# First weight loads on a second queue, scales of three weight chunks from Gram products, and one feed-forward piece in two groups

## The chip, the cores and the metric

The kernel runs on one core of a Trainium2 chip. Its time is device time in microseconds (us): the median of several executions, and before the change three of them gave 1026.77 to 1027.06. A core has five engines that work through their own instruction streams in order: TensorE (PE in the profile; PEld is its weight load), VectorE (DVE), ScalarE (ACT), GpSimd (POOL) and SyncE (SP), which issues most of the DMA transfers. Engines wait for one another by semaphores.

## What is computed

Block-causal attention over 8 batches, 8 heads and 576 positions with heads of 64 (a block of 64 rows sees itself and all blocks before it), and then a feed-forward layer over its output, 4608 tokens of 512.

```python
scores = scale * np.matmul(q, k.transpose(0, 1, 3, 2))
mask = block_i >= block_j                      # blocks of 64
attn = softmax(np.where(mask, scores, -1e9))
x = (attn @ v).transpose(0, 2, 1, 3).reshape(4608, 512)
h = x @ w_in                                   # 512 x 2048
g = h * np.clip(h + 3.0, 0.0, 6.0) / 6.0
out = (g @ w_out).astype(np.float32)           # 2048 x 512
```

q, k and v are float32; the two weight matrices are float64.

## The kernel before

**Precision.** TensorE multiplies fp16 numbers. Nearly every operand is scaled by a power of two, so that its largest element fits, and split into a high and a low fp16 half; a product is three matmuls (high by high, high by low, low by high). The first part of the work is done in plain float32 instead: the attention of batch 0's first 192 rows and the feed-forward of those 192 tokens, since the scales are not known yet.

**Weights.** They come in eight chunks, four loads each (two of `w_in`, two of `w_out`, 512 KB each). A load brings float64 as pairs of 32-bit words into a raw buffer; ScalarE makes `ex` out of the high word, VectorE shifts the low word into `sg` and joins both into float32 in `win` or `wout` (`w_load`, line 605). `w_max` (646) takes the largest magnitude of each chunk: four ScalarE passes with Abs and a running maximum, a transposition on TensorE that brings the 128 partial maxima into a row, a reduction, and a matmul that spreads the result (`pow2_scale`, 529). Its exponent gives the chunk's scale, `pwio`, and the reciprocal, `rsio`. `w_split` (659) writes the two fp16 halves over the float32 of the chunk before. The raw buffers rotate among three places; the constants WX and WY say when the third changes.

**Attention.** A slot is a pair of heads of one batch, 32 in all. Slots 0 to 3 (batch 0) begin in float32 (`qk_prep32`, `s_block32`, `t_block32`, `pv_group32`; tiles `qf`, `qkf`, `sf`, `pf`); the others go through `qk_prep` (767), which takes the absolute maximum of q and k on VectorE (`qkmx`), `s_group` (scores `s`, maxima `st`, exponentials `p`, halves `phl`, transposed by DMA into `pT`) and `pv_group` (1111), which writes the feed-forward's input `x`, one of four buffers `xb`.

**Feed-forward.** 13 pieces: 192 tokens (piece 0), 384, 384, 192, and then nine of 384. A piece has 16 blocks of 128 hidden units. `ffn1_` (1193) makes `h` in one of two PSUM banks, ScalarE's relu gives `r`, VectorE and ScalarE make the two halves of `g`; `ffn2_` (1249) adds g @ w_out to three accumulators `o`, three blocks (LAG) later, and evicts them as `osb` after the sixteenth. The relu needs the scales `eg` (`g_scales`, 674) and `sh` (`h_scale`, 741): they are normed by the largest product of scales over **all eight** chunks. So the relu of piece 1's first block, the first one in fp16, needs the maximum of the last chunk (`need`, 1351, calls `maxes(NCH)`).

**Order.** Nothing above runs in the order of the code. A recorder collects every operation with the tiles it touches (`Recorder.touch`, 195) and a key, a due time out of a table of constants: AS and RT for the float32 slots, AT for the others, FT for the feed-forward, W0 and WD for the weight loads, M0 and MD for the chunk maxima, S0 and SD for the splits. A list scheduler with a cost model (`cost`, 216, `schedule`, 271) then gives each engine its order, and chooses the engine where an operation has several (`scaled` with "AVP"). `emit` (459) issues the instructions, so nearly all carry that line in the trace, and groups are told apart by their tiles.

Of the kernel before, what the change touches and what calls it, by code (L numbers as in the profile page):

```python
# [22 lines left out]
WX = 10  # L23
WY = 27

U = 2.788
AS = (7.494, 11.408, 15.3, 22.633)
AL = 14.807
PV0 = 2.519
TA, TR, PR = 2.197, 5.661, 0.677  # L30
QR = 3.417
PVA, PVB = 0.93, 1.25
# [8 lines left out]
MEM = 0  # L41

NMIN = 64
QL = 0.849
VL = 0.2
W0, WD = 4.938, 2.891
S0, SD = 57.576, 4.59
M0, MD = 34.073, 5
RT = (25.619, 42.369, 59.881, 71.242)
RS, RL, VL1 = 2.796, 15.216, 24.0  # L50
VM0, VMX = 10.452, 0.3
AT = ((4, 86.25), (6, 128.63), (8, 159.32), (10, 199.92), (12, 240.31), (14, 287.79), (16, 335.13), (24, 565.96), (32, 826.62))
# [31 lines left out]
class Recorder:  # L84
# [75 lines left out]

    def load(self, out, in_):

        self.add([(e, "dma_start", (out, in_), {}) for e in self.queues])

    def add(self, ways):
# [8 lines left out]
        else:  # L174
# [15 lines left out]
            self.ops.append(op)  # L190
        for a, w in [(a, False) for a in ins] + [(a, True) for a in outs]:
            if self.on_chip(a):
                self.touch(op, a, w)

    def touch(self, op, a, w):
# [9 lines left out]
        keep = []  # L205
        for e in self.hist.get(t.name, ()):
            o, ow, q0, q1, c0, c1 = e
            inside = p0 <= q0 and q1 <= p1 and b0 <= c0 and c1 <= b1
            if o is not op and (w or ow) and q0 < p1 and p0 < q1 and c0 < b1 and b0 < c1:
                op.preds[o.n] = op.preds.get(o.n, False) or ow and not w  # L210
            if not (w and inside):
                keep.append(e)
        keep.append((op, w, p0, p1, b0, b1))
        self.hist[t.name] = keep

    def cost(self, eng, method, args, kw, outs, ins):
# [3 lines left out]
        if method == "dma_start":  # L220
# [8 lines left out]
            return 600, 2000 + nb / 170, False  # L229
# [41 lines left out]
    def schedule(self):  # L271
# [63 lines left out]
        while done < N:  # L335
# [131 lines left out]
def kernel(  # L467
# [61 lines left out]
    def pow2_scale(mx, n, nm, to=None, exact=False):  # L529
# [26 lines left out]
        nc.vector.tensor_scalar_mul(rs, pw, 1.0 / E_IN)  # L556
        nc.vector.reciprocal(rs, rs)
# [46 lines left out]

    def w_load(w, c, half):
# [52 lines left out]

    def w_split(c):

        rs = rsio[:, c]
        for wi, w in enumerate("io"):
            for half in range(2):
                c32 = w_f32(w, c, half)
                part = w_part(w, c, half)
                hi, lo = (part[:, :, i].rearrange("p r (l n) -> p r l n", l=2) for i in range(2))
                nc.scaled(hi, c32, rs[:, wi:wi + 1], "AVP")
                nc.vector.scalar_tensor_tensor(
                    lo, c32, rs[:, wi:wi + 1], hi, op0=ALU.mult, op1=ALU.subtract
                )  # L670

    gs = []

    def g_scales():

        if not gs:
            pp = sm.tile([P, NCH], F32, tag="pp", name="pp")
            nc.vector.tensor_mul(pp, pwi, pwo)
            m = wpool.tile([P, 1], F32, tag="egm", name="egm")
# [802 lines left out]
```

## Time and profile before

| | |
|---|---|
| median of 3 runs | 1026.9 us (1026.77 to 1027.06) |
| profiled execution, its own time | 1024.76 us |
| span of its profile | 1023.0 us |
| mean granted clock of TensorE | 0.992 |

| engine | busy us | share of the span |
|---|---|---|
| TensorE | 988.8 | 97% |
| VectorE | 821.9 | 80% |
| ScalarE | 624.8 | 61% |
| GpSimd | 61.5 | 6% |

The span runs from the first instruction to the last of the profiled execution. The busy time by stage is cut at the places where TensorE stops being full: the start until 42 us, a gap at 72 to 81, a gap at 128 to 158; behind that TensorE stays busy to the end. Each such row has the stage, its length, then for PE, PEld, DVE, ACT and POOL the busy time and (x) the number of instructions, and at the end the granted clock, the DMA share and GB/s. A row of an engine's timeline has start and length in us, the operation, out<-in, the shapes, and in brackets the idle time ahead of it and what ended that.

### The profile page before, as it was taken

What the parts mean: (1) busy time and instruction counts of PE and PEld (TensorE: products, weight loads), DVE (VectorE), ACT (ScalarE), POOL (GpSimd) and SP (SyncE); (2) the same over time, 40 slices, a digit from 0 to 9 for tenths busy, and PEclk for the clock granted to TensorE, in tenths of its full rate; (3) what the DMA queues carried; (4) which work ended last, traced back from release to release, by engine and by line L of the source; (5) the groups of instructions that cost most, each with busy time, mean ns of one, the idle gap of its engine ahead of it and who ended that gap; (6) DMA issues with size and microseconds to landing.
All of it is one profiled execution on the core that took longest, in us unless ns stands there. A gap on an engine that the chain in (4) does not pass through costs nothing. (4 is left out here: it accounts for less than half of the span.)

```text
span 1023.0 us, 28975 instructions
## 1 busy us (share of the span) xinstructions
PE 988.8 (97%) x11588; PEld 727.2 (71%) x11588; DVE 821.9 (80%) x2311; ACT 624.8 (61%) x1525; POOL 61.5 (6%) x247
## 2 busy tenths in 40 slices
PE   7889989999999999999999999999999999999998
PEld 4656647677777877677767677677777777777776
DVE  4898999999999999998999999887988774232322
ACT  4688766567667766677776675665665653343332
POOL 3211110000000000000000000000000000000000
PEclk9998998999999999999999999999999999999999
DMA  6767755989989998798779788775566352000000
GB/s 157 206 184 210 173 130 97 169 167 182 160 149 180 155 170 162 131 189 145 141 159 159 137 158 155 132 139 90 103 143 103 70 100 35 1 33 2 32 2 32
DMA packets 414200, 128.91 MB, mean 126 GB/s; under 512 B 403184, under 2 KB 403440, under 8 KB 414064
## 3 DMA queue, kind: packets, MB, share of 16 engines
q1 hardware_dynamic: 414064, 127.05, 64.3%
q8 instruction: 91, 1.49, 0.6%
q14 instruction: 45, 0.37, 0.1%
HBM read 45.09 MB, written 9.44 MB: 53 GB/s over the span
## 5 line engine op out<-in xcount | busy, mean ns | idle before, releaser
L463 PE MATMUL h<-x,win 128*64 128x384 f16 (+2 forms) x4720 | 435.9, 321 | 6.2 <-DVE win L463 3.6
L463 PE MATMUL o<-wout,g 128*64 128x512 f16 (+2 forms) x3444 | 428.7, 378 | 0.0
L463 PEld LDWEIGHTS <-win 128*64 128x64 f16 x4608 | 297.6, 110 | 68.6 <-issue 1.7
L463 PEld LDWEIGHTS <-g 128*64 128x64 f16 x3360 | 222.6, 110 | 101.9
L463 ACT ACTIVATE p<-s,st,esc 128x64 f32<-128x64 f32 (+1 forms) x280 | 163.1, 586 | 71.7 <-DVE st L463 56.4
L463 ACT ACTIVATE r<-h,eg,sh 128x384 f32<-128x384 f32 (+1 forms) x240 | 137.2, 592 | 105.7 <-PE h L463 102.9
L463 DVE SCALAR_TENSOR_TENSOR r<-r,eg,h 128x384 f32<-128x384 f32 (+1 forms) x192 | 113.4, 591 | 107.7 <-ACT r L463 107.5
L463 ACT ACTIVATE g<-r 128x384 f16<-128x384 f32 (+1 forms) x163 | 83.2, 511 | 91.2 <-DVE r L463 90.2
L463 DVE SCALAR_TENSOR_TENSOR phl<-p,st,phl 128x128 f16<-128x128 f32 (+4 forms) x252 | 134.9, 582 | 0.2
L463 DVE SCALAR_TENSOR_TENSOR g<-r,g 128x384 f16<-128x384 f32 (+1 forms) x192 | 102.9, 536 | 30.4 <-ACT g L463 29.6
L463 DVE TENSOR_REDUCE st<-s 128x1 f32<-128x64 f32 (+1 forms) x280 | 119.8, 447 | 4.7 <-PE s L463 4.7
L463 PE MATMUL s<-qkT 128*64 128x64 f16 (+7 forms) x1120 | 98.7, 289 | 3.9 <-ACT p L463 2.9
L463 ACT ACTIVATE phl<-p,st 128x256 f16<-128x256 f32 (+4 forms) x122 | 64.2, 556 | 39.6 <-DVE st L463 15.2
L463 PEld LDWEIGHTS <-vhl 128*64 128x64 f16 x1680 | 72.8, 111 | 21.3 <-issue 13.0
L463 PEld LDWEIGHTS <-qkT 128*64 128x64 f16 x1120 | 60.2, 111 | 32.3 <-issue 10.4
L463 PE MATMUL pv<-pT,vhl 128*64 128x192 f16 (+2 forms) x1680 | 74.6, 235 | 8.3 <-DMA pT<-phl 3.2
L463 ACT ACTIVATION_READ_ACCUMULATOR p<-s,st,esc 128x1 f32 x280 | 54.9, 196 | 0.0
L463 POOL MEMSET p<- 128x64 f32 x140 | 21.3, 152 | 518.0 <-DVE phl L463 474.3
L463 DVE TENSOR_SCALAR phl<-p,st 128x512 f16<-128x512 f32 (+4 forms) x130 | 50.0, 418 | 1.7 <-issue 0.3
L463 DVE SCALAR_TENSOR_TENSOR qks<-qk,rs_q,qks 128x576 f16<-128x576 f32 x56 | 44.0, 810 | 0.1
L463 ACT ACTIVATE x<-pv 128x192 f16<-128x192 f32 (+1 forms) x66 | 24.0, 364 | 30.8 <-PE pv L463 27.5
L463 DVE TENSOR_REDUCE qkmx<-qk 128x2 f32<-128x1152 f32 x28 | 37.6, 1344 | 0.8 <-DMA qk<-in_k_dram 0.8
(147 smaller groups left out, 785.5 us busy)
## 6 DMA issues: line engine op xcount, KB each, us to landing
out_dram<-osb SPq DMA_DIRECT2D x35, 256.0 KB, 2.5
vnat<-in_v_dram SPq DMA_DIRECT2D x64, 128.0 KB, 2.8
qk<-in_q_dram SPq DMA_DIRECT2D x28, 288.0 KB, 3.5
qk<-in_k_dram SPq DMA_DIRECT2D x28, 288.0 KB, 4.4
rawo<-in_moe_w_out_dram SPq DMA_DIRECT2D x15, 512.0 KB, 4.0
rawi<-in_moe_w_in_dram SPq DMA_DIRECT2D x14, 512.0 KB, 3.7
pT<-phl SPq DMA_TRANSPOSE x140, 3.5
vnat<-in_v_dram SPq DMA_DIRECT2D x32, 32.0 KB, 2.6
```

The source lines that it names most:

```text
L463: getattr(eng, method)(*args, **kw)
```

## The change

- **Loads.** The first four loads (chunk 0) may go on SyncE's or ScalarE's queue (WQ); the scheduler puts all four on ScalarE's. The table RAWS names the raw buffer of each load, out of six places; the first ten turn through five of them, parts of `xb` among these.
- **Maxima.** For chunks 0 to 2 (GRM) `w_max` no longer uses ScalarE: TensorE multiplies the bf16 upper halves of the float32 weights with themselves (16 matmuls of 128x128 for a chunk, tile `gm`), VectorE takes the diagonal (sums of squares, `wm`), a matmul with ones adds these up (`gs`), and half of that sum's exponent bounds the largest element. Chunks 3 to 7 take two Abs passes of 1024 columns in place of four of 512.
- **Piece 1** is cut into two groups of blocks (GA = 5): the first ten blocks use scales made of chunks 0 to 4 alone; after the tenth the accumulators are evicted into `sofar`, and the last six blocks' result is added to it. `need` asks for five chunk maxima ahead of piece 1, and for all eight ahead of its eleventh block.
- **Shorter chains.** The factor 1/E_IN now comes from the matmul with `one`, so `pow2_scale` and `h_scale` have one VectorE operation less each.
- **Other engines.** The absolute maximum of q and k of slots below 8 (QKA) may go to ScalarE, and the scaled identity `rd` to ScalarE or GpSimd (RDW).
- **Scheduler.** `touch` keeps reads and writes apart; DMA costs are changed; nearly all keys have new values.

Order rows of both kernels follow, at two places. They have the line, the operation, out<-in and the shape; the number behind a tile's name is its allocation.

First place, the program's start, on TensorE. Before (`qt` are transpositions of q and k of the first slot, `sf` its scores):

```order
L463 MATMUL qt_0_110<-ident,qf_106 128x128
L463 MATMUL qt_0_110<-ident,qf_106 128x64
L463 MATMUL qt_1_109<-ident,qf_106 128x128
L463 MATMUL qt_1_109<-ident,qf_106 128x64
L463 MATMUL sf_0_0_116<-qkf_108 128x128
L463 MATMUL sf_1_0_127<-qkf_108 128x128
L463 MATMUL sf_2_0_142<-qkf_108 128x192
L463 MATMUL qt_0_123<-ident,qf_120 128x128
```

In the changed kernel the transpositions of slot 0 and chunk 0's Gram matmuls come first. The last three of these (each with a weight load) and what follows:

```order
L483 LDWEIGHTS wout
L483 MATMUL gm_236<-wout 128x128
L483 MATMUL sf_0_0_119<-qkf_112 128x128
L483 MATMUL qt_1_123<-ident,qf_121 128x128
L483 MATMUL qt_1_123<-ident,qf_121 128x64
L483 MATMUL qt_0_124<-ident,qf_121 128x128
L483 MATMUL qt_0_124<-ident,qf_121 128x64
L483 MATMUL sf_1_0_130<-qkf_112 128x128
```

The first scores (`sf_0_0`) have moved from the place behind four transpositions to that behind the sixteen Gram matmuls, which read the assembled `win` and `wout` of chunk 0.

ScalarE at the same place. Before (`qkf` are the evicted transpositions, `pf` the exponentials):

```order
L463 ACT_TABLE_LOAD
L463 ACTIVATE qkf_108<-qt_0_110 64x3x64
L463 ACTIVATE qkf_108<-qt_1_109 128x192
L463 ACTIVATE pf_0_117,sums_0_114<-sf_0_0_116,st_0_115 128x64
L463 ACTIVATE qkf_121<-qt_0_123 64x3x64
L463 ACTIVATE pT_0_124<-pt_0_0_125 128x128
```

And now:

```order
L483 DMA rawi_0_104<-in_moe_w_in_dram 128x2x512
L483 DMA rawi_1_107<-in_moe_w_in_dram 128x2x512
L483 DMA x_82<-in_moe_w_out_dram 128x1024
L483 DMA x_83<-in_moe_w_out_dram 128x1024
L483 ACT_TABLE_LOAD
L483 ACTIVATE exi_0_106<-rawi_0_104 128x512
L483 ACTIVATE exi_1_109<-rawi_1_107 128x512
L483 ACTIVATE qkf_112<-qt_0_114 64x3x64
L483 ACTIVATE exo_0_116<-x_82 128x512
L483 ACTIVATE exo_1_128<-x_83 128x512
L483 ACTIVATE qkf_112<-qt_1_113 128x192
L483 ACTIVATE qkf_122<-qt_1_123 128x192
```

Four DMA issues (`x_82` and `x_83` are raw buffers in `xb`) stand ahead of the table load, and four `ex` passes stand among the evictions `qkf`.

Second place, VectorE where the scales of piece 1 are made. Before, chunk 7's maximum ends in `am_w`, `pwio` and `rsio`, and `egm`, `rpp`, `eg` and `sh` follow it:

```order
L463 TENSOR_TENSOR pp<-pwio 128x8
L463 RECIPROCAL rsio<-rsio 128x2
L463 TENSOR_REDUCE egm<-pp 128x1
L463 TENSOR_SCALAR win<-x_83,rsio 128x2x256
L463 RECIPROCAL rpp<-egm 128x1
L463 TENSOR_SCALAR wout<-x_84,rsio 128x512
L463 TENSOR_SCALAR eg<-pp,rpp 128x8 x3
L463 SCALAR_TENSOR_TENSOR sh_636<-pwio,pw_v_186,eg 128x8
L463 SCALAR_TENSOR_TENSOR win<-x_83,rsio,win 128x2x256
L463 TENSOR_SCALAR sh_636<-sh_636 128x8
L463 SCALAR_TENSOR_TENSOR win<-x_83,rsio,win 128x2x256
L463 SCALAR_TENSOR_TENSOR wout<-x_84,rsio,wout 128x512
```

Now these operations have 5 columns and come once chunk 4 is done:

```order
L483 TENSOR_SCALAR eg_588<-pp_586,rpp_589 128x5
L483 TENSOR_SCALAR x_82<-rb_2_493,rs_v_188 128x192
L483 TENSOR_SCALAR eg_588<-pp_586,rpp_589 128x5
L483 SCALAR_TENSOR_TENSOR x_82<-rb_2_493,rs_v_188,x_82 128x192
L483 TENSOR_SCALAR am_w_474<-mb_w_477 128x2
L483 TENSOR_SCALAR eg_588<-pp_586,rpp_589 128x5
L483 TENSOR_SCALAR pwio<-am_w_474 128x2
L483 SCALAR_TENSOR_TENSOR sh_5_590<-pwio,pw_v_187,eg_588 128x5
L483 RECIPROCAL rsio<-pwio 128x2
L483 SCALAR_TENSOR_TENSOR so_5_760<-pw_v_187,egm_587 128x1
```

Eleven rows are left out; behind them the scores of slot 4 (`s_0_0_0`) begin:

```order
L483 TENSOR_SCALAR wout<-wout,rsio 128x512
L483 TENSOR_TENSOR sums_2_487<-sums_2_487,st_8_524 128x1
L483 SCALAR_TENSOR_TENSOR wout<-wout,rsio 128x512
L483 TENSOR_SCALAR sums_2_487<-sums_2_487 128x3
L483 TENSOR_REDUCE st_0_551<-s_0_0_0_552 128x1
L483 RECIPROCAL sums_2_487<-sums_2_487 128x3
L483 TENSOR_REDUCE st_0_551<-s_0_0_0_552 128x1 x2
```

Before, slot 4's first three score maxima stood some 80 rows ahead of `sh`; now they stand behind it.

The diff, cut to its core:

```diff
-WX = 10
-WY = 27
+RAWS = (0, 1, 3, 4, 5) * 2 + (0, 1, 4, 5) * 3 + (0, 1, 2) * 2 + (0, 1) * 2
...
+WSP = 2
+LOW = "V"
+WQ = 4
+GA = 5
+GRM = 3
+QKA = 8
+RDW = "PA"
...
-S0, SD = 57.576, 4.59
-M0, MD = 34.073, 5
+S0, SD = 66.989, 3.661
+M0, MD = 32.413, 7.476
...
-        nc.vector.tensor_scalar_mul(rs, pw, 1.0 / E_IN)
-        nc.vector.reciprocal(rs, rs)
+        nc.vector.reciprocal(rs, pw)
...
-        b = len(n_raw) % 3 if len(n_raw) < WY else len(n_raw) % 2
+        b = RAWS[len(n_raw)]
...
+            raw = flat(xb[b - 2], I32)[:, :2 * WC].rearrange("p (n w) -> p n w", w=2)
         n_raw.append(nm)
+        nc.queues = ("sync", "scalar") if len(n_raw) <= WQ else ("sync",)
...
     def w_max(c):
 
-        acc = sm.tile([P, 2, 2], F32, tag="wacc", bufs=2, name=f"wacc{c}")
+        if c >= GRM:
+            m = sm.tile([P, 2], F32, tag="wm", name=f"wm{c}")
+            for wi, w in enumerate("io"):
+                c32 = w_all32(w, c)
+                ab = ffp.tile([P, WC], F32, tag="stage", bufs=NST_B, name=f"ab{w}{c}").bitcast(BF16)
+                ab = ab.rearrange("p (r l n) -> p r l n", r=c32.shape[1], l=2)
+                nc.scalar.activation(ab, c32, AF.Abs, accum_out=m[:, wi:wi + 1])
+            pow2_scale(m, 2, f"w{c}", (pwio[:, c], rsio[:, c]), exact=True)
+            return
+        ps = ps_s.tile([P, 512], F32, tag="s", name=f"gm{c}")
+        nc.joint = "gm", c
         for wi, w in enumerate("io"):
-            for half in range(2):
-                c32 = w_f32(w, c, half)
-                ab = ffp.tile([P, WC], F32, tag="stage", bufs=NST_B, name=f"ab{w}{c}_{half}")
-                ab = ab.rearrange("p (r l n) -> p r l n", r=c32.shape[1], l=2)
-                nc.scalar.activation(ab, c32, AF.Abs, accum_out=acc[:, wi, half:half + 1])
+            t = w_all32(w, c).rearrange("p r l n -> p (r l n)").bitcast(BF16)
+            t = t.rearrange("p (n w) -> p n w", w=2)[:, :, 1]
+            nk = 2 * WC // P
+            for k_ in range(nk):
+                tk = t[:, k_ * P:(k_ + 1) * P]
+                nc.tensor.matmul(ps[:, wi * P:(wi + 1) * P], tk, tk, start=k_ == 0, stop=k_ == nk - 1)
+        nc.joint = None
         m = sm.tile([P, 2], F32, tag="wm", name=f"wm{c}")
-        nc.vector.tensor_reduce(m, acc, axis=AX.X, op=ALU.max)
-        pow2_scale(m, 2, f"w{c}", (pwio[:, c], rsio[:, c]), exact=True)
+        dg = sm.tile([P, P], F32, tag="wdg", bufs=1, name=f"wdg{c}")
+        for wi in range(2):
+            nc.vector.tensor_tensor_reduce(
+                dg, ps[:, wi * P:(wi + 1) * P], ident, 1.0, 0.0,
+                op0=ALU.mult, op1=ALU.add, accum_out=m[:, wi:wi + 1],
+            )
+        ps2 = ps_s.tile([P, 512], F32, tag="s", name=f"gs{c}")
+        nc.joint = "gs", c
+        for h in range(2):
+            nc.tensor.matmul(ps2[h * BLK:(h + 1) * BLK, :2], full1, m, start=True, stop=True)
+        nc.joint = None
+        u = sm.tile([P, 2], F32, tag="wu", name=f"wu{c}")
+        nc.vector.tensor_scalar(
+            u.bitcast(U32), ps2[:, :2].bitcast(U32), 1, EXPONENT_BITS,
+            op0=ALU.logical_shift_right, op1=ALU.bitwise_and,
+        )
+        nc.vector.tensor_scalar(pwio[:, c], u, 2.0 ** 64 / E_IN, TINY, op0=ALU.mult, op1=ALU.max)
+        nc.vector.reciprocal(rsio[:, c], pwio[:, c])
...
+            for r in range(0, R, R // WSP):
+                rr = slice(r, r + R // WSP)
+                nc.scaled(hi[:, rr], c32[:, rr], rs[:, wi:wi + 1], "AVP")
+                nc.resid(lo[:, rr], c32[:, rr], rs[:, wi:wi + 1], hi[:, rr], LOW)
...
+    def g_scales(n=NCH):
...
+            nc.vector.tensor_mul(pp, pwi[:, :n], pwo[:, :n])
...
+    def g_group(pc, f):
+
+        return GA if pc == 1 and f * NCH // NFT < GA else NCH
...
-        absmax(mx, t)
+        ways = [("vector", "tensor_reduce", (mx, t), dict(axis=AX.XY, op=ALU.max, apply_absolute_value=True))]
+        if n < QKA:
+            ways.append(("scalar", [
+                ("activation", (sp[:, 2].rearrange("p t l d -> p (t l d)")[:, :NST * D].rearrange("p (t d) -> p t d", d=D), t[:, s], AF.Abs), dict(accum_out=mx[:, s:s + 1]))
+                for s in range(2)
+            ]))
+        nc.add(ways)
...
-            nc.gpsimd.tensor_scalar(rd[:, i], ident2, r[:, i:i + 1], 1.0, op0=ALU.mult, op1=ALU.mult)
+            nc.scaled(rd[:, i], ident2, r[:, i:i + 1], RDW)
...
+        cut = not last and g_group(pc, f) != g_group(pc, f + 1)
+        first = first or g_group(pc, f) != g_group(pc, f - 1)
+        last = last or cut
...
+        if cut:
+            so = out_scales(pc, g_group(pc, f))
+            for t, a in enumerate(acc[pc]):
+                nc.scaled(sofar[:, t], a, so[:, t:t + 1], "AV")
+            acc[pc] = [ps_o.tile([P, DM], F32, tag=f"o{t}", name=f"o{pc}_{t}b") for t in range(nt)]
...
+            if pc == 1 and GA < NCH:
+                nc.vector.scalar_tensor_tensor(
+                    oc, ac, so[:, t:t + 1], sofar[:, t], op0=ALU.mult, op1=ALU.add
+                )
+            else:
+                nc.scaled(oc, ac, so[:, t:t + 1] if pc else 1.0 / 6.0, "AV")
...
-        maxes(NCH)
+        maxes(NCH if pc > 1 or c >= GA else GA)
```

More of the change, by code (lines that the diff above doesn't have):

```diff
@@ L159, in scaled, with resid @@
         self.add(ways)
+    def resid(self, out, in_, scale, hi, engines):
+        self.add([
+            ("vector" if e == "V" else "gpsimd", "scalar_tensor_tensor", (out, in_, scale, hi),
+             dict(op0=ALU.mult, op1=ALU.subtract))
+            for e in engines
+        ])
     def load(self, out, in_):
@@ L190, in add @@
             self.ops.append(op)
+        for _, *call in ways[1:]:
+            for _, a, k in call[0] if isinstance(call[0], list) else [call]:
+                more, _ = self.operands(a, k)
+                outs = outs + [x for x in more if all(x is not y for y in outs)]
         for a, w in [(a, False) for a in ins] + [(a, True) for a in outs]:
@@ L204, in touch @@
             op.tiles.append(t.name)
[L205 to L214, printed above, removed]
+        writes, reads = self.hist.setdefault(t.name, ([], []))
+        for kind in (writes, reads) if w else (writes,):
+            keep = []
+            for e in kind:
+                o, q0, q1, c0, c1 = e
+                if o is not op and q0 < p1 and p0 < q1 and c0 < b1 and b0 < c1:
+                    op.preds[o.n] = op.preds.get(o.n, False) or kind is writes and not w
+                if not (w and p0 <= q0 and q1 <= p1 and b0 <= c0 and c1 <= b1):
+                    keep.append(e)
+            if w:
+                kind[:] = keep
+        (writes if w else reads).append((op, p0, p1, b0, b1))
     def cost(self, eng, method, args, kw, outs, ins):
@@ L603, in w_f32, with w_all, w_all32 @@
         return t.rearrange("p (r l n) -> p r l n", r=NDT // 2 if w == "i" else 1, l=2)
+    def w_all(w, c):
+        if w == "i":
+            return win[:, c]
+        return wout[:, 2 * c:2 * c + 2]
+    def w_all32(w, c):
+        if c + 1 < NCH:
+            return w_all(w, c + 1).bitcast(F32)
+        t = flat(xb[2 if w == "i" else 3], F32)[:, :2 * WC]
+        return t.rearrange("p (r l n) -> p r l n", r=NDT if w == "i" else 2, l=2)
     def w_load(w, c, half):
@@ L662, in w_split @@
         for wi, w in enumerate("io"):
[L663 to L679, printed above, removed]
+            c32 = w_all32(w, c)
+            part = w_all(w, c)
+            hi, lo = (part[:, :, i].rearrange("p r (l n) -> p r l n", l=2) for i in range(2))
+            R = c32.shape[1]
+            for r in range(0, R, R // WSP):
+                rr = slice(r, r + R // WSP)
+                nc.scaled(hi[:, rr], c32[:, rr], rs[:, wi:wi + 1], "AVP")
+                nc.resid(lo[:, rr], c32[:, rr], rs[:, wi:wi + 1], hi[:, rr], LOW)
+    gs = {}
+    def g_scales(n=NCH):
+        if n not in gs:
+            pp = sm.tile([P, n], F32, tag=f"pp{n}", bufs=1, name=f"pp{n}")
+            nc.vector.tensor_mul(pp, pwi[:, :n], pwo[:, :n])
+            m = wpool.tile([P, 1], F32, tag=f"egm{n}", name=f"egm{n}")
             nc.vector.tensor_reduce(m, pp, axis=AX.X, op=ALU.max)
-            t = wpool.tile([P, 3, NCH], F32, tag="eg", name="eg")
-            r = sm.tile([P, 1], F32, tag="rpwi", name="rpp")
+            t = wpool.tile([P, 3, n], F32, tag=f"eg{n}", name=f"eg{n}")
+            r = wpool.tile([P, 1], F32, tag=f"rpp{n}", name=f"rpp{n}")
             nc.vector.reciprocal(r, m)
@@ L1128, in pv_group @@
             if pc in (2, 3):
[L1129 removed]
+                need(NPC, NCH - 1)
         t = pT.pop((n, g))
```

91 lines of the change are left out of this document (46 added, 45 removed).

## The prediction

> **What bounds the kernel now.** I read the page's first lines, then cut the span into stages by their busy times, then read each engine's timeline where a stage shows TensorE idle. The page's totals first.
>
> ```profile
> span 1023.0 us, 28975 instructions
> ...
> PE 988.8 (97%) x11588; PEld 727.2 (71%) x11588; DVE 821.9 (80%) x2311; ACT 624.8 (61%) x1525; POOL 61.5 (6%) x247
> ```
>
> TensorE (PE) is idle for 1023.0 - 988.8 = 34.2 us in all, so a change that keeps its work cannot gain much more than that, plus what a throttled clock costs. The busy time by stage (length, then PE, PEld, DVE, ACT, POOL busy, then granted clock, DMA share, GB/s) says where those 34 us lie.
>
> ```profile
> 0.00:5.80 5.80, 1.65 (x4) 0.75 (x5) 1.31 (x7) 1.94 (x3) 4.77 (x19) 1.00 0.33 75
> 5.80:14.00 8.20, 7.40 (x24) 4.83 (x24) 3.69 (x12) 3.26 (x17) 2.67 (x12) 1.00 0.45 102
> 14.00:28.00 14.00, 11.96 (x48) 7.63 (x48) 6.91 (x21) 6.11 (x26) 2.67 (x7) 1.00 0.92 247
> 28.00:42.00 14.00, 11.26 (x69) 7.47 (x66) 11.41 (x36) 11.29 (x34) 3.12 (x8) 1.00 0.77 205
> 42.00:72.00 30.00, 29.74 (x178) 19.37 (x176) 28.20 (x75) 23.72 (x62) 5.74 (x11) 1.00 0.63 184
> 72.00:81.00 9.00, 4.08 (x16) 2.81 (x18) 8.08 (x19) 7.17 (x19) 0.72 (x1) 0.69 0.66 195
> 81.00:128.00 47.00, 46.95 (x303) 31.18 (x299) 43.45 (x119) 37.43 (x98) 8.85 (x21) 0.99 0.74 189
> 128.00:147.00 19.00, 16.77 (x121) 9.71 (x123) 18.92 (x66) 12.97 (x36) 2.43 (x7) 0.91 0.61 136
> 147.00:158.00 11.00, 6.35 (x71) 4.03 (x66) 11.00 (x36) 8.05 (x18) 1.72 (x4) 0.81 0.60 128
> 158.00:400.00 242.00, 239.44 (x3312) 183.69 (x3313) 239.79 (x718) 163.34 (x407) 11.22 (x62) 0.99 0.90 158
> ...
> 840.00:1010.00 170.00, 169.58 (x1868) 128.90 (x1864) 56.69 (x103) 61.64 (x117) 0.00 (x0) 1.00 0.08 18
> ```
>
> Three places hold most of it. The **start** (0 to 42) leaves PE idle for 4.15 + 0.80 + 2.04 + 2.74 = 9.7 us. **Hole B** (72 to 81) has 4.92 us idle and, at a clock of 0.69, loses another 9 x 0.31 = 2.8 us: 7.7 us. **Hole A** (128 to 158) has 2.23 + 4.65 us idle and 19 x 0.09 + 11 x 0.19 = 3.8 us of clock: 10.7 us. From 158 to 400 PE and VectorE (DVE) are both full, DVE for 239.79 of 242; from 840 on PE runs alone. So the end is PE's work plus these holes, and an earlier arrival at 158 is kept.
>
> **What the holes wait for.** TensorE's timeline (start, length; in brackets the idle time before it and what ended it), then VectorE's and ScalarE's (ACT):
>
> ```profile
> 75.38 1.65 PE L463 MATMUL h<-x,win 128*128 128x192 f32 x4 [3.56 <-DVE win L463]
> 78.57 1.01 PE L463 MATMUL h<-x,win 128*128 128x192 f32 x2 [1.54 <-DVE g L463]
> ...
> 155.12 1.40 PE L463 MATMUL s<-qkT 128*64 128x64 f16 x16 [1.65 <-ACT p L463]
> ```
>
> ```profile
> 74.65 0.67 DVE L463 SCALAR_TENSOR_TENSOR win<-exi,sgi 128x512 uint32<-128x512 uint32 x1
> ...
> 143.71 0.40 DVE L463 SCALAR_TENSOR_TENSOR x<-rb,rs_v,x 128x192 f16<-128x192 f32 x1
> ...
> 155.17 0.22 DVE L463 SCALAR_TENSOR_TENSOR sh<-pwio,pw_v,eg 128x8 f32<-128x8 f32 x1
> ```
>
> ```profile
> 140.14 0.62 ACT L463 ACTIVATE abo<-x 128x512 f32<-128x512 f32 x1
> ...
> 156.17 1.23 ACT L463 ACTIVATE r<-h,eg,sh 128x384 f32<-128x384 f32 x2 [0.34 <-DVE sh L463]
> ```
>
> Hole B: the f32 feed-forward of piece 0 waits for the assembly of chunk 3's weights (`win`), which DVE ends at 75.3. Hole A: the first relu of piece 1 waits for `sh`, the scales that need the maxima of all eight chunks; the last maximum starts on ScalarE at 140.14, and its chain through PE and DVE ends at 156.2. Piece 1's input x was complete at 143.71 + 0.40 = 144.1. Both `h` banks are held meanwhile, so PE has only scraps of attention to run.
>
> **The change part by part.** *Hole A.* The scales of piece 1's first ten blocks need chunks 0 to 4 alone, and they now stand in DVE's order ahead of slot 4's scores (the second place shown with the change). The 16 us chain leaves the path. Next late is x: the relu could start about 2 us after 144.1, 10 us earlier. The chain's own part is the stage from 147 to 158, 4.65 us of idle time and 2.1 us of clock; of the 3.9 us before it, waits for a loaded DVE, I take half. -8.7 us (bounds 0 and -10.7).
>
> *Hole B.* Chunk 3's assembly moves ahead in DVE's order: 35 us of DVE work stand before it where there were 50, summed from the start-to-start times of before. The wait of 3.56 us and the slow clock behind it go; next late is `g`, whose 1.54 us may stay in part. -7.0 us (bounds -3 and -7.7).
>
> *Start.* Four weight loads leave SyncE's queue and stand on ScalarE's, ahead of its table load, and chunk 0's 16 Gram matmuls stand in PE's order ahead of the first scores (the first place). Behind the waiting Gram matmuls are the scores, and so the exponentials; on ScalarE the q and k evictions queue behind `exo`, on DVE behind `win`.
>
> ```profile
> 5.81 1.83 PE L463 MATMUL sf<-qkf 128*128 128x128 f32 x6 [0.47 <-issue]
> ```
>
> ```profile
> rawi<-in_moe_w_in_dram SPq DMA_DIRECT2D x14, 512.0 KB, 3.7
> ```
>
> Four loads are 2.1 MB; the first 14 us of before moved 5.8 x 75 + 8.2 x 102 = 1.3 MB of q, k and v. At the 247 GB/s of 14 to 28 the weights alone take 8.5 us, all of it 13.8 us. With 0.7 us until the first issue and 3.2 us for prelu, assembly and Gram (an estimate: 0.7 + 0.7 + 1.8), the first scores come at 12.4 to 17.7, against 5.81. I take 14.4, 8.6 us late. Part is made up: between 14 and 42 PE had 4.8 us of idle time and DVE was busy for 18.3 of 28 us. +4.5 us (bounds -2, if earlier loads shorten that stretch as well, and +16, if nothing is made up and the rate is worse).
>
> The Trainium skill (Trainium Kernel Development and Optimization, Key Constraints) says that the queues of several engines share the same 16 DMA engines and save only issue time. By that rule, which speaks against this move, ScalarE's queue brings no bandwidth, and the q, k and v loads slow down beside it. No run here shows two queues yet.
>
> *Gram work.* 48 matmuls of 128x128 in bf16 have no row. Between these lies their price:
>
> ```profile
> 105.70 0.82 PE L463 MATMUL pt<-ident,pf 128*128 128x128 f32 x6
> 106.35 0.82 PE L463 MATMUL h<-x,win 128*128 128x192 f32 x4
> ...
> 857.46 2.15 PE L463 MATMUL h<-x,win 128*64 128x384 f16 x24
> 859.41 2.14 PE L463 MATMUL o<-wout,g 128*64 128x512 f16 x18
> ```
>
> An f32 pass of 128 columns takes 0.65 / 6 = 0.11 us. In f16, 24 halves of 384 columns take 1.95 us, 0.16 us for a full array, so 0.05 us for 128 columns. 2.6 to 5.2 us; being 16 bit, nearer to the low end: 3.0, less 0.7 us for three transposed maxima: +2.3 us (bounds 1.9 and 4.5).
>
> *The cut in piece 1, and the shorter chains.*
>
> ```profile
> L463 ACT ACTIVATE osb<-o,so 128x512 f32<-128x512 f32 x28 | 18.2, 687 | 5.9 <-PE o L463 5.7
> L463 DVE TENSOR_REDUCE qkmx<-qk 128x2 f32<-128x1152 f32 x28 | 37.6, 1344 | 0.8 <-DMA qk<-in_k_dram 0.8
> L463 DVE TENSOR_SCALAR rs_q<-pw_q 128x2 f32<-128x2 f32 x28 | 4.4, 156 | 0.1
> ```
>
> Three more evictions of 0.69 us stand between the tenth block's output and the next group's. In PE's order a whole `h` block of 1.95 us lies between and hides them: +0.5 us; without that cover 2 us. DVE loses 28 x 0.156 us of `rs_q`, four `qkmx` of 1.34 us and some 50 small ones, about 16 us, and gains about 5 us (Gram diagonals, a second set of scales, piece 1's sums). ScalarE takes some of it over and is at 61%. In the stage from 158 to 400, where DVE is full, PE idles for 2.56 us: -1.0 us (bounds -2.6 and +1).
>
> **The sum**: -8.7 - 7.0 + 4.5 + 2.3 + 0.5 - 1.0 = -9.4 us. The profiled execution took 1024.76 us (the span of 1023.0 and 1.8 around it), which gives 1015.4. The median of the runs lies 2.1 us above that execution: 1017.5.
>
> **Rivals.** *1, slower: the start comes too late.* If the five-buffer loads share badly and get two thirds of 247 GB/s, 3.4 MB take 20.6 us, the first scores come at 24.5, 18.7 us late, and none of it is made up, since the f32 slots 0 to 3 follow one another through the same tiles. 18.7 + 2.3 + 0.5 - 16.7 = +4.8: 1031.7. It decides from a first score near 20 on. For it: at 247 GB/s the DMA share is 0.92 already, and three engines queue behind these loads. Against it: one load alone lands 3.7 us after its issue.
>
> *2, no change: paid back.* The start loses its 8.6 us in full, Gram 4.5, the cut 2, while Hole A shrinks by 8 and Hole B by 7: about 0, 1027. For it: DVE was busy for 18.92 of 19 us ahead of 147, so PE may meet DVE where it met `sh`. Against it: DVE has less to do before that point.
>
> *3, a smaller gain: a cold PE.*
>
> ```profile
> 8.77 0.45 PE L463 MATMUL pt<-ident,pf 128*128 128x128 f32 x1 [0.32 <-ACT pf L463]
> ...
> 29.46 0.27 PE L463 MATMUL pt<-ident,pf 128*128 128x128 f32 x1
> ```
>
> One transposition takes 0.45 us early and 0.27 us later: PE starts slow, though the first stages' rows say 1.00. If the wait before the Gram matmuls keeps it slow for 10 us more, 5 us go: 1022.5. The Trainium skill (TensorE: Matmul & The Clock Gate, Part 1) states half rate after an idle window of about 3.4 us. The trace agrees in Hole B, 3.56 us of waiting and a clock of 0.69.
>
> **How the numbers follow.** Forecast 0.64, rival 1 0.12, rival 2 0.13, rival 3 0.11. A measurement of this kernel can tell about 0.2%, 2 us, from no change. Forecast and rival 3 are faster (0.75), rival 2 is the same (0.13), rival 1 slower (0.12). The forecast's own range is 1008 to 1023. The low end of mine, 1005, puts the better bounds of all terms together; the high end, 1028, takes in rivals 2 and 3 and leaves rival 1 out.
>
> **What would show it.** In the changed profile: first scores between 12 and 18; no wait of `h` for `win` above 1 us; a first relu of piece 1 before 150, not ended by `sh`; PE idle for about 28 us; from 840 on the same 1.95 us for a block. A first score past 20, a new PE wait of several us around piece 1's start or its cut, or DVE idle for more than 5 us between 160 and 400 would make me wrong.

## The result

| | median us | runs | lowest to highest us | ratio to before (95% interval) |
|---|---|---|---|---|
| before | 1026.98 | 4 | 1026.77 to 1027.61 | |
| changed | 1011.55 | 4 | 1009.56 to 1014.19 | 0.985 [0.9826, 0.9874] |

The changed kernel is 15.4 us faster; 9.4 were forecast. Its profiled execution took 1014.19 us, the longest of its four, and that of before 1024.76, 2.2 below its median, so the two profiles are only 10.6 us apart. All medians and ratios here are of executions in the faster state alone, and three slow ones are left out, two of the kernel before with the new DMA cost (1035.68 and 3572.29 us) and one with the keys of before (2054.22). The profile's totals after the change:

```profile
span 1012.4 us, 28927 instructions
...
PE 981.3 (97%) x11633; PEld 708.9 (70%) x11633; DVE 814.0 (80%) x2256; ACT 630.7 (62%) x1528; POOL 54.1 (5%) x227
```

TensorE's idle time has hardly moved: 1012.4 - 981.3 = 31.1 us, against 34.2. The stages show why. After the change, with the columns of the first table of stages (length; PE, PEld, DVE, ACT, POOL busy; clock, DMA share, GB/s):

```profile
0.00:42.00 42.00, 29.59 (x155) 19.39 (x156) 29.78 (x88) 26.85 (x86) 11.21 (x38) 0.88 0.83 237
42.00:72.00 30.00, 30.00 (x208) 21.17 (x207) 26.73 (x74) 25.56 (x61) 4.33 (x7) 1.00 0.91 283
72.00:81.00 9.00, 8.93 (x60) 5.88 (x59) 8.58 (x26) 8.05 (x21) 2.65 (x5) 1.00 0.44 94
81.00:128.00 47.00, 47.00 (x312) 30.83 (x312) 44.67 (x136) 38.50 (x104) 5.35 (x12) 1.00 0.59 129
128.00:158.00 30.00, 30.00 (x337) 18.02 (x338) 29.07 (x87) 22.39 (x56) 2.69 (x9) 1.00 0.67 121
158.00:180.00 22.00, 22.00 (x275) 16.66 (x271) 22.00 (x71) 14.86 (x37) 1.07 (x6) 1.00 0.79 153
180.00:400.00 220.00, 210.09 (x2927) 157.74 (x2925) 207.91 (x610) 152.36 (x376) 9.54 (x54) 0.99 0.91 159
```

The same two ends of the table before the change:

```profile
0.00:42.00 42.00, 32.27 (x141) 20.68 (x142) 23.32 (x74) 22.60 (x77) 13.23 (x44) 1.00 0.70 181
...
180.00:400.00 220.00, 217.47 (x3064) 167.08 (x3062) 218.52 (x660) 150.31 (x377) 10.46 (x57) 1.00 0.94 165
```

Both holes are gone: from 42 to 180 TensorE is idle for 0.07 us. The idle time that is left stands ahead of them and behind them. The start has 12.4 us in place of 9.7, and from 180 to 400 there are 9.9 us where there were 2.5. VectorE is *less* busy there than before (207.91 against 218.52), so it did not simply fill up. From 160 to 400, before and then after:

```profile
160.00:400.00 240.00, 237.47 (x3302) 182.25 (x3300) 237.85 (x713) 162.55 (x405) 11.22 (x62) 1.00 0.91 159
```

```profile
160.00:400.00 240.00, 230.09 (x3175) 173.02 (x3172) 227.91 (x667) 165.21 (x408) 10.62 (x60) 0.99 0.91 160
```

VectorE is idle for 12.1 of these 240 us. The prediction had named over 5 us there as a sign that it is wrong, and that sign came; another, TensorE idle for about 28 us in all, came out at 31.1.

**One scale for all runs.** Idle time and clock have to be added up by hand, so the tables below use one number, TensorE's *loss* up to a time t: t, less the price of all matmuls begun by t. A matmul's price is the mean start-to-start time of its shape in the kernel before, at full clock and without a pause (a Gram matmul at 0.055 us, half an f32 pass). Idle time, a slow clock and stretched matmuls all count as loss; the kernel's own work doesn't. Read the differences between kernels: the level depends by some 2 us up to 400, and by 5 at the end, on how the mean of a shape is taken, and the last row of the next table by 0.3 at most.

| loss up to (us) | 42 | 72 | 81 | 128 | 158 | 180 | 400 | end |
|---|---|---|---|---|---|---|---|---|
| before | 22.3 | 22.2 | 29.2 | 29.8 | 41.9 | 43.0 | 48.1 | 55.9 |
| changed | 22.2 | 22.1 | 22.2 | 22.3 | 23.6 | 23.7 | 38.1 | 43.3 |
| difference | -0.1 | -0.2 | -7.0 | -7.5 | -18.2 | -19.3 | -9.9 | -12.7 |

Added work of 2.1 us (the Gram matmuls, less three transposed maxima) brings the last difference to the 10.6 us between the spans. So in this profile 19.3 us were won by 180, and half of it was given back by 400. It is that of the longest execution; the next profile gives back less.

The first relu of piece 1, on ScalarE's timeline, comes 22 us earlier (156.17 before), and no scale ends its wait:

```profile
133.88 0.66 ACT L483 ACTIVATE r<-h,eg,sh 128x384 f32<-128x384 f32 x1
```

### The profile page after: what moved, and what is told of

Its sections match the earlier page's. It is cut to its first block, busy times and chain, and to the rows that moved or that the text cites. A ratio compares the mean times of both kernels' runs of the same rounds, so it can differ in the third digit from the quotient of the medians.

```text
span 1012.4 us, 28927 instructions
## 1 busy us (share of the span) xinstructions
PE 981.3 (97%) x11633; PEld 708.9 (70%) x11633; DVE 814.0 (80%) x2256; ACT 630.7 (62%) x1528; POOL 54.1 (5%) x227
## 5 line engine op out<-in xcount | busy, mean ns | idle before, releaser
L483 PE MATMUL h<-x,win 128*64 128x384 f16 (+2 forms) x4720 | 431.5, 320 | 1.1 <-DVE r L483 1.1
L483 PE MATMUL o<-wout,g 128*64 128x512 f16 (+3 forms) x3336 | 412.6, 379 | 0.0
L483 PEld LDWEIGHTS <-win 128*64 128x64 f16 (+1 forms) x4632 | 292.8, 110 | 79.0 <-issue 3.9
L483 PEld LDWEIGHTS <-g 128*64 128x64 f16 x3360 | 216.5, 110 | 110.4 <-issue 0.2
L483 DVE SCALAR_TENSOR_TENSOR phl<-p,st,phl 128x384 f16<-128x384 f32 (+4 forms) x252 | 136.6, 583 | 2.5 <-ACT phl L483 2.4
L483 DVE SCALAR_TENSOR_TENSOR g<-r,g 128x384 f16<-128x384 f32 (+1 forms) x192 | 103.0, 537 | 30.4 <-ACT g L483 29.9
L483 ACT ACTIVATE phl<-p,st 128x256 f16<-128x256 f32 (+4 forms) x136 | 72.3, 566 | 26.6 <-DVE st L483 10.9
L483 PEld LDWEIGHTS <-qkT 128*64 128x64 f16 x1120 | 55.2, 110 | 30.5 <-issue 9.2
L483 DVE TENSOR_SCALAR phl<-p,st 128x128 f16<-128x128 f32 (+4 forms) x116 | 44.2, 414 | 2.7 <-DVE st L483 0.5
L483 DVE TENSOR_REDUCE qkmx<-qk 128x2 f32<-128x1152 f32 x24 | 32.2, 1343 | 4.4 <-DMA qk<-in_k_dram 4.4
L483 DVE TENSOR_SCALAR st<-st,esc 128x3 f32<-128x3 f32 (+1 forms) x168 | 34.5, 212 | 0.9
```

The source lines that it names most:

```text
L483: getattr(eng, method)(*args, **kw)
```

## The experiments

All were timed beside the kernel before; it had medians of 1027.25 to 1027.94 us there.

| run | median us | ratio (95% interval) | loss up to 42 | 81 | 180 | 400 | end |
|---|---|---|---|---|---|---|---|
| the change again | 1010.29 | 0.9833 [0.9807, 0.986] | 22.4 | 22.2 | 23.8 | 31.9 | 39.4 |
| one group in piece 1 | 1015.18 | 0.9888 [0.9871, 0.9904] | 22.0 | 22.2 | 31.6 | 38.6 | 44.3 |
| no Gram products | 1009.88 | 0.9835 [0.9815, 0.9856] | 22.9 | 22.6 | 24.3 | 34.8 | 39.2 |
| no second queue | 1013.09 | 0.9863 [0.9844, 0.9882] | 21.6 | 22.1 | 24.2 | 38.6 | 43.8 |
| keys of before | 1018.02 | 0.9916 [0.99, 0.9931] | 23.3 | 23.4 | 29.7 | 41.0 | 50.3 |
| three raw buffers | 1011.46 | 0.9847 [0.9834, 0.986] | 24.1 | 25.7 | 25.9 | 35.3 | 39.3 |
| dense matmuls first | 1013.24 | 0.987 [0.9857, 0.9882] | 22.8 | 22.9 | 24.3 | 34.7 | 42.5 |
| later p times v | 1011.63 | 0.9845 [0.9832, 0.9857] | 25.5 | 25.4 | 26.5 | 37.1 | 42.9 |
| **before**, new DMA cost | 1017.3 | 0.9896 [0.9876, 0.9915] | 19.4 | 19.9 | 34.2 | 36.2 | 48.3 |
| named parts undone | 1015.51 | 0.9889 [0.9869, 0.9909] | 16.5 | 18.0 | 29.9 | 36.5 | 43.4 |
| the same, two groups | 1009.84 | 0.9821 [0.9802, 0.984] | 16.7 | 18.0 | 28.0 | 36.0 | 39.1 |
| q, k maxima on ScalarE | 1009.31 | 0.9822 [0.9801, 0.9843] | 22.0 | 22.2 | 23.6 | 30.4 | 36.9 |

### The change again

The same kernel, with more runs.

> The changed kernel once more. Theory: its runs spread (1009.6 to 1014.2) because the profiled one had a spell at half clock of 10.2 us right behind the first Gram matmuls and the others hardly any (mean clock 0.993 against 0.999 and 1.0). Then a run of about 1010 shows no such spell, and TensorE's loss up to 42 us is about 5 us smaller, with the later stages unchanged. Rival: the runs differ in the crowded stage from 158 to 400 us, by DMA; then the loss up to 42 us is the same in a faster run. Median expected 1011, between 1009.5 and 1014.

The clock theory fell. The 1010.29 us execution that was profiled has no half-clock record at the start, and still the loss up to 42 us is 22.4. The two profiles part between 180 and 400: 14.5 us of loss in the one, 8.1 in the other. So the kernel before lost 5.1 us in this stage, and the change loses 9.4 or 3.0 more. That is the spread of this kernel, and a difference of a few us in that stage between two single profiles says nothing. VectorE is idle for 6.4 us from 160 to 400 in this profile.

### One group in piece 1

```diff
-GA = 5
+GA = 8
```

> Piece 1 in one group again (GA = 8), the rest of the change kept: its first relu needs all eight maxima. If the cut is what closed the gap at 128 to 158 us, that gap comes back, 8 to 11 us by 180 us. Then two theories part: if the 9 us that the changed kernel loses again between 200 and 400 us are a limit of that stage (VectorE and the DMA engines), the late arrival is not paid there and the time is 1011 to 1015; if they are waits of one particular order, the time is 1019 to 1023. Rival on the cut: the maxima come early enough without it, gap below 3 us, time 1010 to 1013.

The gap came back: its stage from 128 to 158 (same columns) has 4.7 us idle at a clock of 0.89.

```profile
128.00:158.00 30.00, 25.32 (x235) 16.70 (x235) 27.23 (x77) 15.81 (x36) 2.24 (x6) 0.89 0.55 113
```

By 180 the loss is 7.8 us above that of the change; at the end 4.9 are left in the profiles, and 4.9 in the medians. So in this kernel the cut is worth 5 us, and the time lies at the upper end of the first range: part of the late arrival is not paid.

### No Gram products; no second queue

```diff
-GRM = 3
+GRM = 0
```

> All chunk maxima from ScalarE's Abs passes (GRM = 0), the loads still on ScalarE's queue. By the terms of the prediction the Gram products cost 2.3 us of work and most of the 4.5 us at the start: 1004 to 1008, with the first scores near 6 us. Rival: the dense burst of 16 matmuls brings TensorE to full clock at 13 us, where the kernel before stays slow until about 27 us, and the short Gram chain frees ScalarE; then taking it away costs 2 to 8 us: 1013 to 1019, and the transpositions at 14 to 27 us take 0.45 us in place of 0.27.

Neither came: 1009.88 is the change's time within 0.2%. The first scores still come at 10.77 us, and TensorE's timeline of this run names the reason, the load of k:

```profile
9.46 0.85 PE L483 MATMUL qt<-ident,qf 128*128 128x128 f32 x2 [2.31 <-DMA qf<-in_k_dram]
```

The next run, without the second queue, has k's first transposition at 4.24 us:

```profile
4.24 0.47 PE L483 MATMUL qt<-ident,qf 128*128 128x128 f32 x1 [0.38 <-DMA qf<-in_k_dram]
```

SyncE issues these loads of k at 2.0 us in both runs. So the weight loads on ScalarE's queue make k land 5 us later, and the Gram matmuls add hardly 2.

```diff
-WQ = 4
+WQ = 0
```

> All loads on SyncE's queue (WQ = 0); the scheduler then puts the first four behind q, k and v, and chunk 0's Gram matmuls come later, the first scores near 6 us. If the early loads are what closed the gap at 72 to 81 us, 3 to 7 us of waiting for win come back: 1014 to 1019. If they only delay the first scores, the start gets shorter and nothing comes back: 1006 to 1010. If the start is made up for anyway, 1010 to 1013.

The first scores come at 5.70 us again, yet the loss at 42 is 21.6, and nothing comes back at 72 to 81. 1013.09 is 2.8 us above the change's 1010.29, but the two intervals overlap. So neither the early loads nor the Gram products close the first gap, and the lateness of the first scores by itself costs nothing by 42 us.

### Keys of before; three raw buffers

The first puts back all due times that the change moved (AS, PV0, QR, W0, M0, S0, RT, AT, FT and the rest), the second the rotation of raw buffers:

```diff
-RAWS = (0, 1, 3, 4, 5) * 2 + (0, 1, 4, 5) * 3 + (0, 1, 2) * 2 + (0, 1) * 2
+RAWS = (0, 1, 3) * 3 + (0, 1, 2) * 6 + (1, 0) * 2 + (1,)
```

> The change with the keys of the kernel before (loads, maxima, splits, slots, feed-forward as they were due then), all its new code kept. The gap at 72 to 81 us stayed closed without the cut, without Gram products and without the second queue, so what closed it is the keys or the raw buffers. If the keys: TensorE's loss grows by 5 to 7 us again between 72 and 81, and the time is 1014 to 1020. If the buffers or the other edits: no step there, and 1009 to 1013.

> The change with the three raw buffers of the kernel before in place of five and four. If the buffers closed the gap at 72 to 81 us (loads could start earlier), 3 to 7 us come back there: 1014 to 1018. If the keys did it, no step at 72 to 81 and 1009 to 1012.

Still no step between 72 and 81 (23.6 to 23.4 with the old keys, 25.3 to 25.7 with three buffers). The old keys cost 7.7 us all the same, in other places: 5.9 us of loss by 180, over half of it in the second gap, and 10.9 at the end of the profile, which is that of its longest run. That the new keys are worth this only beside the other new parts is seen below.

### What closed the first gap

No part that has a name in the change had closed it. The order of the kernel before shows something odd at this place. On VectorE, with the allocation numbers, which rise in the order of the code (300 and 315 are chunk 3's halves of `w_in`, 370 and 377 chunk 4's):

```
142 L463 SCALAR_TENSOR_TENSOR win<-exi_0_300,sgi_0_299 128x512
148 L463 SCALAR_TENSOR_TENSOR win<-exi_1_377,sgi_1_376 128x512
155 L463 SCALAR_TENSOR_TENSOR win<-exi_1_315,sgi_1_314 128x512
```

Chunk 4's second half is assembled before chunk 3's, which TensorE is waiting for. The timeline of before shows the price, the last row being the one that ends TensorE's 3.56 us:

```profile
72.22 0.67 DVE L463 SCALAR_TENSOR_TENSOR win<-exi,sgi 128x512 uint32<-128x512 uint32 x1
...
74.65 0.67 DVE L463 SCALAR_TENSOR_TENSOR win<-exi,sgi 128x512 uint32<-128x512 uint32 x1
```

The kernel before, with one thing of the change:

```diff
-            return 600, 2000 + nb / 170, False
+            return 600, 2000 + nb / (290 if nb >= 400000 else 210), False
...
-                nb = (took - (2900.0 if e == "gpsimd" else 2000.0)) * 0.8
+                nb = took - (2900.0 if e == "gpsimd" else 2000.0)
```

> The kernel before with one thing of the change: the scheduler's cost of a DMA transfer. In the order of the kernel before, chunk 4's second w_in half stands ahead of chunk 3's second half, in SyncE's queue and in VectorE's assembly; with the new cost it stands behind it. Theory: the gap at 72 to 81 us is this inversion, which explains why no part that was undone alone brought it back; then 5 to 7 us of TensorE's loss between 72 and 81 go and the later gap stays: 1020 to 1023. Rival: the gap is VectorE's load at that place and needs the work that the change takes off it; then TensorE waits for the next assembly instead, 1025 to 1028.

It did better than expected: 1017.3, 10.6 us faster. With the new cost VectorE assembles 315 before 377 (in SyncE's queue 375 still stands ahead of 313, so that half of the expectation was wrong), and the first gap is gone, while the second stays:

```profile
72.00:81.00 9.00, 8.46 (x61) 5.76 (x57) 8.72 (x24) 8.46 (x23) 4.64 (x7) 1.00 0.78 203
81.00:128.00 47.00, 43.63 (x273) 28.25 (x272) 44.85 (x128) 37.25 (x102) 9.33 (x21) 0.96 0.61 155
128.00:158.00 30.00, 25.63 (x250) 16.54 (x248) 28.61 (x86) 20.46 (x48) 3.09 (x9) 0.94 0.74 134
```

VectorE is as busy from 72 to 81 as it was (8.72 of 9 us, 8.08 before), so it is not relief that closes the gap; the rival is out. The cost also reorders other loads, and 2.9 us of loss go before 42. That the inversion alone makes the gap is therefore likely, not isolated.

### The named parts undone, and the cut alone

The change with WQ = 0, GRM = 0, QKA = 0, RDW = "P", the three raw buffers and the keys of before; once with GA = 8 and once with GA = 5.

> The change without its named parts: no second queue, no Gram products, three raw buffers, piece 1 in one group, the maxima of q and k on VectorE, rd on GpSimd, and the keys of the kernel before. What is left is the scheduler's costs, the shorter scale chains and Abs passes of 1024. Theory: the gap at 72 to 81 us is closed by the costs alone, the one at 128 to 158 stays, 12 us less at most 2: 1018 to 1022. Rival: the parts back each other up, and with all of them gone the first gap is back too: 1024 to 1028.

> As the run without the named parts, but piece 1 in two groups (GA = 5). Theory: the two groups alone take 7 to 11 us of the gap at 128 to 158 us, of which 2 to 3 are given back between 180 and 400: 1011 to 1015. Rival: without the early maxima five chunks come too late as well, the gap keeps over 7 us: 1016 to 1020.

1015.51 is below the range: the costs, the separate reads and writes of `touch`, the shorter chains and the longer Abs passes alone take 12.4 us. That is 1.8 us more than the DMA cost alone took, and the two intervals overlap. With the two groups added it is 1009.84, which is the whole change's time. So the DMA cost and the cut carry nearly all of it, and second queue, Gram products, buffers, the maxima of q and k on ScalarE and the new keys together are worth nothing that can be measured. The stages of the run with two groups:

```profile
0.00:42.00 42.00, 34.70 (x168) 23.40 (x168) 26.29 (x82) 26.11 (x83) 12.31 (x45) 1.00 0.76 208
...
128.00:158.00 30.00, 25.79 (x274) 17.55 (x274) 28.74 (x82) 18.29 (x44) 2.01 (x8) 0.94 0.66 134
...
180.00:400.00 220.00, 214.85 (x3033) 166.56 (x3029) 219.75 (x651) 153.18 (x380) 10.90 (x60) 1.00 0.83 166
```

At the start TensorE is busy for 34.70 us where the changed kernel has 29.59, and 5.5 us of loss are missing: that is what the named parts, the new keys among them, together cost there. But the second gap is still 4.2 us of idle time and a clock of 0.94, so the expectation's mechanism was wrong and its time came out slightly better than its range: the cut takes 1.9 us of loss by 180, and the rest of its 5.7 us comes later. It isn't the scales that are missing: the first relu of piece 1 runs at 135.57, 1.7 us behind the changed kernel's, and no scale ends its wait (in the run without the cut `sh` still does, at 141.57). What TensorE waits for is VectorE's second `r`, and ahead of that stand splits of weights:

```profile
146.05 3.75 PE L483 MATMUL h<-x,win 128*64 128x384 f16 x24 [2.36 <-DVE r L483]
```

```profile
140.91 1.33 DVE L483 TENSOR_SCALAR win<-x,rsio 128x512 f16<-128x512 f32 x2
142.15 1.40 DVE L483 SCALAR_TENSOR_TENSOR win<-x,rsio,win 128x512 f16<-128x512 f32 x2
143.47 1.40 DVE L483 SCALAR_TENSOR_TENSOR wout<-x,rsio,wout 128x512 f16<-128x512 f32 x2
...
145.40 0.60 DVE L483 SCALAR_TENSOR_TENSOR r<-r,eg,h 128x384 f32<-128x384 f32 x1
```

The run with the keys of before alone has the same six splits ahead of the same `r`, and a wait of 1.98 us:

```profile
149.19 1.03 PE L483 MATMUL h<-x,win 128*64 128x384 f16 x6 [1.98 <-DVE r L483]
```

The runs without Gram products, second queue or five buffers, which have the new keys, are idle for 1.03 us at most from 128 to 158. So this rest of the second gap comes with the old keys, an order once more, and not with late maxima. No run moves the splits alone, so that the splits make it is likely, not isolated.

### Dense matmuls at the start

```diff
+    wz = sm.tile([P, P], BF16, tag="wz", bufs=1, name="wz")
+    nc.vector.memset(wz, 0.0)
+    wps = ps_s.tile([P, 512], F32, tag="s", name="warm")
+    for i in range(64):
+        nc.tensor.matmul(wps[:, :P], wz, wz, start=i == 0, stop=i == 63)
```

> The change with 64 matmuls of 128x128 bf16 zeros ahead of everything on TensorE, whose result nothing reads (added work of some 3 to 7 us, while the queue waits for q and k). TensorE loses 22 us up to 42 us in every kernel so far, 10 to 12 of them idle; the rest is matmuls that take 0.45 us in place of 0.27. Theory: that is a clock which rises only after dense work, and these matmuls raise it: transpositions at 13 to 27 us take 0.27 to 0.33 us, the loss up to 42 us falls by 3 to 8, the time to 1003 to 1008. Rival: the early matmuls are slow for another reason, or the clock falls again in the waits that follow: loss unchanged within 1.5 us, time 1009 to 1013.

The rival was right, though its range ended at 1013, and its second half is the reason. TensorE's timeline of this run:

```profile
1.70 6.30 PE L483 MATMUL warm<-wz 128*128 128x128 bf16 x64 [1.70 <-DVE wz L483]
...
10.11 0.63 PE L483 MATMUL gm<-win 128*128 128x128 bf16 x8
...
13.88 0.33 PE L483 MATMUL pt<-ident,pf 128*128 128x128 f32 x1
17.77 1.19 PE L483 MATMUL sf<-qkf 128*128 128x128 f32 x4 [3.56 <-ACT pf L483]
18.75 0.42 PE L483 MATMUL pt<-ident,pf 128*128 128x128 f32 x1
```

Eight Gram matmuls take 0.63 us (1.03 in the changed kernel at this place) and a transposition 0.33: the clock did rise. Then comes a wait of 3.56 us for ScalarE, and the next transposition takes 0.42 again; the granted clock is 0.50 from 17.4 to 27.4. The loss at 42 is 22.8, with no price given to the 64 added matmuls.

### What is given back from 180 on

```diff
-PVA, PVB = 1.039, 1.474
+PVA, PVB = 1.1, 1.6
```

> The change with the products of p and v due later (PVA 1.039 to 1.1, PVB 1.474 to 1.6 slots behind their scores). Between 180 and 400 us the changed kernel gives back 8 to 14 us, and the longest waits there are pv for pT, the transposing DMA. Theory: these are waits of an order that puts pv ahead of its transfer; later ones have the wait under 1 us in all and give back 3 to 6 us less: 1005 to 1008. Rival: the stage is limited by its throughput, so the wait shows up on another operation and the time stays 1009 to 1013.

TensorE's waits from 180 to 400 (us in total, times, longest), of the changed kernel and then of this run:

```profile
PE pv L483 <- DMA pT<-phl: 4.8, 4, 2.2
PE s L483 <- DVE x L483: 1.5, 1, 1.5
PE mb_q L483 <- DVE dg_v L483: 1.4, 1, 1.4
```

```profile
PE pv L483 <- DMA pT<-phl: 1.9, 2, 1.2
PE pv L483 <- ACT p L483: 1.5, 2, 1.2
PE o L483 <- DVE osb L483: 1.0, 1, 1.0
PE h L483 <- DVE r L483: 1.0, 2, 0.5
```

The wait for the transposing DMA is shorter (it is 2.9 us in the second profile of the change) and others took its place; 10.6 us are given back, 1011.63. The rival holds.

```diff
-QKA = 8
+QKA = 32
```

> The change with the absolute maxima of q and k of all slots free to go to ScalarE (QKA = 32): 19 of VectorE's 24 reductions of 1.34 us move, some 25 us, and ScalarE gets 38 passes. Theory: what is given back between 180 and 400 us is VectorE's throughput; then TensorE's loss there falls from 8 to 14 us to about 5, and the time to 1003 to 1007. Rival: it is the length of the chains through ScalarE, the transposing DMA and VectorE; then the loss stays or grows, since ScalarE's queue gets longer: 1009 to 1015.

6.8 us are given back, and the time is 1009.31. VectorE lost 10 us of busy time (803.8 against 814.0), ScalarE gained 19. The same changed kernel gave back 8.1 and 14.5 in two profiles, so this is at most a hint of VectorE's part; the medians cannot be told apart, and the time lies in the rival's range.

The column at 400 says the most. At 180 the twelve runs and the two kernels differ by 19 us (23.6 to 43.0); at 400 all changed ones lie between 30.4 and 41.0, and a kernel that came to 180 ten us later than the change (the new DMA cost alone, 34.2) is at 36.2 against its 31.9 and 38.1. So some of what comes early is waited away here: the profiles with a loss of up to 26.5 at 180 lose 6.8 to 14.4 us in this stage, those with 28.0 and more lose 2.0 to 11.3. That is a tendency of single profiles with a wide spread. What sets this pace, the chain through scores, exponentials, transposing DMA and p times v, or VectorE inside it, is not settled.

## Why the prediction came out as it did

| step | forecast | measured (loss or work, us) |
|---|---|---|
| Hole A | -8.7 | -12.3 (81 to 180) |
| Hole B | -7.0 | -6.9 (72 to 81) |
| start | +4.5 | -0.2 (to 72) |
| Gram work | +2.3 | +2.1 (by its price) |
| cut | +0.5 | no wait for it above 0.2 us |
| chains, later stages | -1.0 | +9.4 (180 to 400), -2.7 (from 400) |
| sum | -9.4 | -10.6 (the profiles) |

The medians are 15.4 us apart, since the profiled execution is the slowest of the changed kernel; in the second profile (1010.29 us) the same row is +3.0 from 180 to 400 and -0.3 from there on. That -9.4 and -10.6 are close is luck: Hole A and the start came out 3.6 and 4.7 us better, the late stages 7.7 us worse, and these errors cancel. The price of the Gram work is borne out at full clock, where eight of these matmuls start within 0.47 us; chunk 0's need 0.83 us for eight, and the scale counts the rest of that as loss.

**Hole A.** Right in mechanism, and larger. "Next late is x" at 144 was wrong: everything ahead of x had moved too, and the first relu ran at 133.9. The run with one group shows that the cut is needed for it (7.8 us by 180), the run with the cut alone that it does not suffice: what is left there is VectorE's order, with splits ahead of `r`.

**Hole B.** Right in place and size, "chunk 3's assembly moves ahead in DVE's order". Why it moves was not asked: the scheduler's cost of a DMA transfer, half a sentence in the list of the change, does it alone and won 10.6 us in the kernel before. The prediction gave it no term.

**Start.** The first scores came at 12.36 us, the early bound of 12.4 to 17.7: the loads ran at up to 408 GB/s there and not at 247. What they waited for was not the weights. TensorE's last wait is for k, and the Gram matmuls follow without one:

```profile
9.86 0.88 PE L483 MATMUL qt<-ident,qf 128*128 128x128 f32 x2 [2.49 <-DMA qf<-in_k_dram]
10.68 1.03 PE L483 MATMUL gm<-win 128*128 128x128 bf16 x8
```

The rule of the Trainium skill that the prediction set against the move (Trainium Kernel Development and Optimization, Key Constraints: the queues share the DMA engines) held: k came 5 us later beside the second queue. All of the delay was made up by 42. But "+4.5" had no term on the other side. The run with the cut alone shows both: the new costs and shorter chains win 5.6 us of loss at the start, the named parts together lose 5.5. Of queue, Gram products, buffers and keys none alone, undone, brought it back, so which one costs is open.

**Chains.** The step that failed. Less VectorE work was to shorten a stage in which VectorE is full (-1.0), and "an earlier arrival at 158 is kept". VectorE did get less work, and TensorE waits more: +9.4 us of loss from 180 to 400 in one profile, +3.0 in the other, with VectorE idle for 12.1 and 6.4 us. So of the 19 us won by 180, 10 to 16 are kept at 400. That the stage has a pace of its own, and that the earlier arrival is what makes it wait, fits most runs and is not shown. It is like the second rival's mechanism, "paid back", at another place: not where `sh` was, but behind it.

**The rivals.** The late start was to decide from a first score near 20 us on, and it was at 12.4. (The 3.7 us that it took for one load alone are the median of fourteen loads, most of them with others beside them.) The slow clock at the start is there, as the third rival had it (a transposition still takes 0.42 us at 24 us), but just as long before the change, so it moved nothing. The Trainium skill (TensorE: Matmul & The Clock Gate, Part 1) has the rate halved after some 3.4 us without work; the dense run agrees, 3.56 us of waiting and 0.33 back to 0.42 us. But a wait that long is not needed. In the changed kernel a transposition takes 0.33 us at 14.9 and 0.42 at 17.1, the granted clock is 0.50 from 16.8 to 27.1, and the only wait of TensorE above 0.2 us between 10 and 17 us is one of 1.00.

## What to carry to other kernels

Where a scheduler sets the order, read the order around a wait before looking for work to take away: here two assemblies stood the wrong way round, and a changed cost in the model was worth more than a second queue and a new algorithm. Undoing parts one at a time hides what they do together; build the opposite kernel as well, all undone but one. And ask what pace the next stage has before counting an early arrival: of nineteen us, three in one profile and nine in the other ended as waits there.

## Not expected of the hardware

The granted clock reads 1.00 until its first record, which comes 7 to 28 us into the span, and a 1.00 there is no measurement. The stage from 0 to 42 has 0.88 in one profile of the changed kernel and 1.00 in the other, with 29.59 and 30.02 us busy, the same loss, and transpositions of 0.42 us near 24 us in both.

The DMA rate of the changed kernel, 40 slices of its first 30 us:

```profile
GB/s 0 0 63 145 376 399 403 392 339 408 368 286 236 156 90 52 135 208 93 175 188 175 194 65 84 94 148 97 51 88 60 192 177 84 202 391 412 388 421 410
```

While loads of 512 KB run, it is 339 to 408 GB/s between 3 and 8 us, on two queues, and 388 to 421 from 26 to 30 us, on SyncE's alone. In this kernel the rate goes with the large loads and not with the number of queues; the 247 GB/s that the prediction used came from a stretch with small q, k and v loads among them.
